# Products of the unit matrix in TensorE's queue, ahead of the first transposes and of those of ten early tiles

## The chip, the core and the metric

The kernel runs on one core of a Trainium2 chip. A core has five engines, each with its own queue of instructions that it takes in order: TensorE (PE in the profile; its weight loads are PEld) multiplies matrices, VectorE (DVE) and ScalarE (ACT) work element by element and can read the results of PE in PSUM, GpSimd (POOL) works element by element on SBUF, and SyncE (SP) issues the DMA transfers here. The metric is the time of one execution on the device, in microseconds, as the median of several runs.

## The reference

Attention with a threshold, followed by a two-layer network. The shapes are 8 batches, 8 heads, 576 rows and 64 columns per head; the network takes 4608 rows of 512, with a hidden width of 2048.

```python
scores = scale * np.matmul(q, k.transpose(0, 1, 3, 2))
thresh = np.max(scores, axis=-1, keepdims=True) - tau
scores = np.where(scores >= thresh, scores, -1000000000.0)
scores = scores - np.max(scores, axis=-1, keepdims=True)
attn = np.exp(scores)
attn = attn / (np.sum(attn, axis=-1, keepdims=True) + 1e-09)
x = np.matmul(attn, v)          # heads side by side: 4608 x 512
h = x @ w_in                    # 512 x 2048
g = np.maximum(h, 0.0) + np.log1p(np.exp(-np.abs(h)))
out = g @ w_out                 # 2048 x 512
```

## The kernel before

**Attention.** A unit is one batch and one pair of heads; there are 32 units of nine tiles of 128 query rows, so 288 tiles, numbered from 0. Each tile goes through the same steps. `scores` (line 425) multiplies on PE into one of two PSUM banks `s`; `row_max` (446) takes the largest score on DVE into `negm` and the threshold `thr`; `exps` (453) takes exponentials on ACT into `e_all`, which has room for two tiles; `mask` (457) drops what lies under the threshold on DVE and sums the row; `weights_T` (477) transposes the masked tile on PE against the unit matrix `ident`; `weights_hi` (512) copies the transposed tile out of PSUM on ACT into `gH`; `values` (561) multiplies by v on PE. For the first 36 tiles the transposes go into the pool of four PSUM banks with tag `g` (line 483), later into the tile's own bank of scores. Beside this the next unit's k and q are split into a rounded part and a rest on POOL (`hi_of`, `lo_of`, lines 124 to 133), transposed on PE (`qkT`, 370) and copied out by ACT; the halves of qT are swapped by DMA (lines 404 and 405).

**Weights.** w_in and w_out are 64-bit numbers in DRAM and arrive in pieces of 512 KB. `to_f32` (169) turns each piece into a pair of 32-bit words: DMA into `wc` (line 204), ACT takes the high word's size into `wa` (212), POOL clamps it (213), three DVE steps put the bits together (219 to 224), and POOL makes the rounded part and the rest (196 and 197). Pieces of w_in are then written back to DRAM as `wi_d` by DMA (line 253), and pieces of w_out stay in SBUF as `wo`. Each piece needs free buffers before its load can start.

**Network.** Nine chunks of 512 rows. `hidden` (651) makes the hidden layer in three products per block (lines 664, 666 and 668), ACT takes the softplus, and `project` (720) multiplies by w_out (line 732). The first chunk can start when the four units of batch 0, tiles 0 to 35, have stored their x.

**Order.** The loop at line 963 calls these steps tile by tile in the order of the letters of `PAT0` (tiles before 36) and `PAT` (after). That is the order in which the program is written down. Where each instruction then stands in its engine's queue is settled by the scheduler of the framework when the program is built: it places instructions by its own estimate of when each could run, within their dependencies and within the order that `behind` (143) adds as a dependency without a wait. So code that is added on one engine can move instructions on all of them.

Of the kernel before, what the change touches and what calls it, by code (L numbers as in the profile page):

```python
# [9 lines left out]
F32 = mybir.dt.float32  # L10
# [13 lines left out]
P = 128  # L24
# [9 lines left out]
PAT = "ThRlefmpfxSvwp"  # L34
PAT0 = "RMTeShlfpfxvwp"
WD = 4
ST = (1, 3, 4, 4, 5, 6, 6, 8)
VO = (1, 1, 1, 0)
RT = 1
# [21 lines left out]
def tile_kernel(ctx: ExitStack, tc: tile.TileContext, q, k, v, tau, w_in, w_out, out):  # L61
# [8 lines left out]
    nc = tc.nc  # L70
# [19 lines left out]
    ps_g = ctx.enter_context(tc.tile_pool(name="ps_g", bufs=GB, space=PSUM))  # L90
# [5 lines left out]
    identr = cpool.tile([P, P], F32R, name="identr")  # L96
# [41 lines left out]

    now = {"p": 0, "tile": 0}
    masked = []  # L140
    scored = []

    def behind(i, others):

        if others:
            tc.add_manual_dep(i.ins, others[-1].ins.name, mybir.DependencyInfo(
                mybir.DependencyClass.NoSync, mybir.DependencyReason.DATA), reason="order")
# [146 lines left out]
    for b in range(B):  # L294
        for kind in (("one", "two") if b < NSPLIT else ("all",)):
            for hp in range(NPAIR):
# [6 lines left out]
                for g, (j, members) in enumerate(groups):  # L303
                    c = 0
# [65 lines left out]
    def qkT(s, j, n):  # L370

        ps = ps_g.tile([P, 512], F32, tag="g", name=f"tr_{s.i}_{j}_{n}")
        pr = ps.bitcast(F32R)
        if n == 2:
            nc.tensor.transpose(pr[:, 0:P], s.k2[:, NC, :], identr)
            if j == 0 and s.kind != "one":
                nc.tensor.transpose(pr[:, P:2 * P], s.q2[0][:, NC, :], identr)
            defer(1, lambda: qkT_rest(s, j, ps))
            return
        cols = range(NC) if n == 0 else range(NC)[s.cols]  # L380
        for c in cols:
            src = s.k2[:, j * (NC + 1) + c, :] if n == 0 else s.q2[j][:, c, :]
            nc.tensor.transpose(pr[:, c * P:(c + 1) * P], src, identr)  # L383
        if n == 0:
            s.kT.append(apool.tile([P, S + SR], F32R, tag="kT", name=f"kT_{s.i}_{j}"))
            t = s.kT[j]
            defer(1, lambda: act.copy(t[:, SR:S], ps))
        else:
            t = [apool.tile([P, SM], F32R, tag=f"qT{i}", name=f"qT{i}_{s.i}_{j}") for i in range(2)]
            s.qT.append(t)  # L390
            w = slice(cols[0] * P, (cols[-1] + 1) * P)
            defer(1, lambda: queries(s, t[0][:, w], t[1][:, w], ps[:, w]))
# [32 lines left out]
    def scores(s, t):  # L425
        if t == s.tiles[0]:
            s.sums = apool.tile([P, 9], F32, tag="sums", name=f"sums_{s.i}")
            s.half, s.sp, s.m, s.grp = {}, {}, {}, {}
        sp = banks[nth[0] % SB]
        s.half[t] = half = nth[0] % 2  # L430
        nth[0] += 1
        s.sp[t] = sp
        if t == NC:
            parts = [(qm[:, n, j, :], j) for j in range(2) for n in range(2)]
        else:
            j = 0 if t < NC else 1
            c = t if t < NC else t - NC - 1
            parts = [(s.qT[j][n][:, c * P:(c + 1) * P], j) for n in range(2)]
        k0 = (1 - half) * SR
        for m, (lhs, j) in enumerate(parts):  # L440
            for hf in range(2):
                i = nc.tensor.matmul(sp[:, hf, 0:HS], lhs, s.kT[j][:, k0 + hf * HS:k0 + (hf + 1) * HS],  # L442
                                     start=(m == 0), stop=(m == len(parts) - 1))
        scored.append(i)

    def row_max(s, t):
        negm = apool.tile([P, 1], F32, tag="negm", bufs=3, name=f"negm_{s.i}_{t}")
# [22 lines left out]
    def mate(s, t):  # L470
# [3 lines left out]
        u = t if t < NC else t - 1  # L474
        return (t + 1, False) if u % 2 == 0 else (t - 1, True)

    def weights_T(s, t):
        half = s.half[t]
        e = e_all[:, half, :]
        other, second = mate(s, t)  # L480
        lone = other is None
        if 9 * NPAIR * s.b + 9 * s.hp + t < TG:
            main = ps_g.tile([P, NC, P], F32, tag="g", name=f"tm_{s.i}_{t}")
            rest = ps_g.tile([P, NC, P], F32, tag="g", name=f"tr_{s.i}_{t}")[:, 0, :] if lone or second else None
        else:
            sp = s.sp[t]
            main = sp[:, 0, :].rearrange("p (c n) -> p c n", n=P)
            rest = sp[:, 1, 0:P]
        if second:
            nc.tensor.transpose(rest, e_all.rearrange("p h n -> p (h n)")[:, SM:SM + P], ident)  # L490
        for c in range(NC):
            c0 = half * SR + c * P
            nc.tensor.matmul(main[:, c, :], e[:, c0:c0 + P], ident, is_transpose=True, start=True, stop=True)  # L493
        if lone:
            r0 = 0 if half else SM
            nc.tensor.transpose(rest[0:SR, :], e[:, r0:r0 + SR], ident)
        s.sp[t] = (main, rest)
# [53 lines left out]
    def slow_products():  # L551
        if not slow:
            return
        for f in slow[0][:3]:
            behind(f(), scored)
        del slow[0][:3]
        if not slow[0]:
            slow.pop(0)
            defer(1, ends.pop(0))
# [289 lines left out]
    chunks, first = [], []  # L849
# [26 lines left out]
    for kind, g in WL:  # L876
        for m in range(4):
            n = len(prep)
# [56 lines left out]


    u0 = units[0]
    for s in units:
        s.eng_lo = nc.gpsimd
    load(u0)  # L940
# [22 lines left out]
    for g, (cur, t) in enumerate(tiles):  # L963
# [6 lines left out]
        for step in PAT0 + ("m" if g == TG - 1 else "") if g < TG else PAT:  # L970
# [24 lines left out]
            elif step == "w":  # L995
                while prep and prep[0][0] <= g:
                    _, f, a = prep.pop(0)
# [42 lines left out]
```

## Time and profile before

| | |
|---|---|
| median of three runs | 1426.15 us (1426.09 to 1426.85) |
| profiled execution, its own time | 1425.26 us |
| its span, first to last instruction | 1423.5 us |
| PE busy | 1380.4 us, 97% of the span |
| DVE, ACT, POOL busy | 69%, 59%, 41% |
| granted TensorE clock, mean | 1.000 |

The page gives busy time per engine, the chain of work that ended last, and the costliest groups of instructions. The windows split the span into stretches, since a mean over the whole hides that the first 145 us, before the network starts, are a different stage from the rest. The timelines show single instructions with the idle time before them and what ended it. Names are those of the kernel's tiles without their numbers. Helpers record under one line: all DVE and ACT operations read as L156 and need their tile's name.

### The profile page before, as it was taken

Reading aid. Unit: us, or ns where it says so; the run is one execution under the profiler, and the core shown is the slowest. Engines: PE = TensorE matmul, PEld = TensorE weight load, DVE = VectorE, ACT = ScalarE, POOL = GpSimd, SP = SyncE. Lnnn points to the kernel's source line nnn. Section 1 sums busy time; section 2 is a strip of 40 time slices with the busy share of each in tenths; the row PEclk is TensorE's granted clock in tenths of the full one; section 3 lists DMA queues with packets and bytes.
Section 4 is the critical chain, followed back from the end, with each engine's and each line's share of the span. In section 5 each row is a group of like instructions: output and inputs, shape, how many; then the busy total and the mean of one; then the engine's idle time right before and its main releaser. Section 6 shows DMA issues by size and latency. Waiting matters only on the chain.

```text
span 1423.5 us, 23587 instructions
## 1 busy us (share of the span) xinstructions
PE 1380.4 (97%) x7860; PEld 1164.5 (82%) x7860; DVE 987.5 (69%) x2211; ACT 846.7 (59%) x1615; POOL 586.2 (41%) x619
## 2 busy tenths in 40 slices
PE   6987999999999999999999999999999999999998
PEld 5555688788888888888888888888888888788886
DVE  6988688787777777787778777877777777402111
ACT  5766767667666576667666666667666765221110
POOL 3666666543333433344334333344334431323221
PEclk9999999999999999999999999999999999999999
DMA  5766766435333534445443533453434532343421
GB/s 168 220 191 208 233 195 186 125 102 173 111 105 111 156 105 124 120 131 158 118 119 98 158 108 110 124 145 117 123 113 141 154 94 84 110 130 115 135 76 45
DMA packets 131209, 189.94 MB, mean 133 GB/s; under 512 B 35312, under 2 KB 86800, under 8 KB 131088
## 3 DMA queue, kind: packets, MB, share of 16 engines
q1 hardware_dynamic: 131088, 188.43, 45.4%
q8 instruction: 63, 1.03, 0.3%
q14 instruction: 58, 0.48, 0.1%
HBM read 140.51 MB, written 27.41 MB: 118 GB/s over the span
## 4 chain that ended last, share of the span: by engine, by line
PE 86%; DVE 4%; DMA 2%; issue 2%; POOL 2%; ACT 1%; SPq 1%; POOLq 0%; DVEq 0%; ACTq 0%
PE o L732 28%; PE s L442 11%; PE h L664 9%; PE h L666 9%; PE h L668 9%; PE s L493 7%; PE pv L574 4%; PE pv L575 4%; PE tr L383 2%; DVE e_all L156 1%; PE pv L576 1%; DVE negm L156 1%; PE s L490 1%; PE pv L568 1%; DMA wc_i<-in_moe_w_in_dram 1%
## 5 line engine op out<-in xcount | busy, mean ns | idle before, releaser
L732 PE MATMUL o<-wo_o,g 128*128 128x512 f32 x1728 | 446.4, 400 | 1.1 <-POOL g L133 1.1
L732 PEld LDWEIGHTS o<-wo_o,g 128*128 128x128 f32 x1728 | 313.7, 189 | 60.6 <-POOL g L133 2.1
L133 POOL TENSOR_TENSOR g<-st,g 128x512 fp32r<-128x512 f32 x144 | 189.8, 1338 | 240.4 <-DVE g L156 222.4
L156 DVE SCALAR_TENSOR_TENSOR e_all<-s,thr,e_all 128x576 f32<-128x576 f32 x288 | 235.2, 817 | 38.0 <-ACT e_all L156 33.4
L156 ACT CAST gH<-s 128x512 fp32r<-128x512 f32 (+2 forms) x432 | 179.5, 467 | 136.8 <-PE s L493 115.5
L156 ACT ACTIVATE e_all<-s,negm 128x576 f32<-128x576 f32 x288 | 215.8, 750 | 32.7 <-DVE negm L156 17.0
L664 PE MATMUL h<-xh,wi 128*128 128x512 f32 x576 | 232.6, 404 | 1.8 <-ACT xh L156 0.8
L156 DVE TENSOR_REDUCE negm<-s 128x1 f32<-128x576 f32 x288 | 215.2, 747 | 25.0 <-PE s L442 21.9
L666 PE MATMUL h<-xl,wi 128*128 128x512 f32 x576 | 231.6, 402 | 0.7 <-POOL xl L133 0.7
L668 PE MATMUL h<-xh,wi 128*128 128x512 f32 x576 | 229.2, 398 | 0.0
L156 DVE TENSOR_TENSOR gL<-s,gH 128x512 fp32r<-128x512 f32 (+1 forms) x270 | 169.0, 634 | 47.3 <-ACT gH L156 40.5
L442 PE MATMUL s<-kT,qT 128*128 128x288 f32 x1024 | 193.0, 311 | 8.1 <-ACT gH L156 4.1
L156 DVE CAST g<-st 128x512 fp32r<-128x512 f32 x128 | 58.8, 501 | 169.0 <-ACT st L156 169.0
L442 PEld LDWEIGHTS s<-kT,qT 128*128 128x128 f32 x1024 | 148.4, 191 | 24.6 <-ACT gH L156 5.3
L493 PE MATMUL s<-identr,e_all 128*128 128x128 f32 x1008 | 151.3, 273 | 0.2 <-DVE e_all L156 0.2
L156 ACT ACT_TABLE_LOAD x111 | 142.4, 1283 | 5.4 <-PE h L668 3.4
L156 ACT ACTIVATE st<-h 128x512 f32<-128x512 f32 x144 | 78.3, 595 | 112.5 <-PE h L668 111.8
L664 PEld LDWEIGHTS h<-xh,wi 128*128 128x128 f32 x576 | 108.5, 188 | 25.7 <-ACT xh L156 1.3
L493 PEld LDWEIGHTS s<-identr,e_all 128*128 128x128 f32 x1008 | 119.4, 140 | 10.9 <-DVE e_all L156 3.5
L666 PEld LDWEIGHTS h<-xl,wi 128*128 128x128 f32 x576 | 108.6, 188 | 22.2 <-POOL xl L133 1.5
L668 PEld LDWEIGHTS h<-xh,wi 128*128 128x128 f32 x576 | 108.5, 188 | 22.1
L574 PE MATMUL pv<-gH,vt 128*128 128x256 f32 (+1 forms) x432 | 118.3, 297 | 0.3 <-ACT gH L156 0.2
(94 smaller groups left out, 1830.0 us busy)
## 6 DMA issues: line engine op xcount, KB each, us to landing
wi<-wi_d SPq DMA_DIRECT2D x144, 512.0 KB
qT<-qT SPq DMA_DIRECT2D x124, 128.0 KB
R<-r_d SPq DMA_DIRECT2D x64, 144.0 KB
kn<-in_k_dram SPq DMA_DIRECT2D x32, 256.0 KB
qn<-in_q_dram SPq DMA_DIRECT2D x32, 256.0 KB
vn<-in_v_dram SPq DMA_DIRECT2D x32, 256.0 KB
wc_i<-in_moe_w_in_dram SPq DMA_DIRECT2D x16, 512.0 KB
wi_d<-wc_i SPq DMA_DIRECT2D x32, 256.0 KB
```

The lines of the kernel that those rows point to most:

```text
L133: eng.tensor_tensor(out=out_, in0=in_, in1=hi.bitcast(F32), op=ALU.subtract)
L156: i = getattr(self.eng, name)(*args, **kwargs)
L383: nc.tensor.transpose(pr[:, c * P:(c + 1) * P], src, identr)
L442: i = nc.tensor.matmul(sp[:, hf, 0:HS], lhs, s.kT[j][:, k0 + hf * HS:k0 + (hf + 1) * HS], start=(m == 0), stop=(m == len(parts) - 1))
L490: nc.tensor.transpose(rest, e_all.rearrange("p h n -> p (h n)")[:, SM:SM + P], ident)
L493: nc.tensor.matmul(main[:, c, :], e[:, c0:c0 + P], ident, is_transpose=True, start=True, stop=True)
L574: nc.tensor.matmul(o[:, 0:n], vt[:, c, :], h[:, c, 0:n], start=(c == 0), stop=False)
L575: nc.tensor.matmul(o[:, 0:n], vt[:, c, :], l[:, c, 0:n], start=False, stop=False)
L664: nc.tensor.matmul(h, wi[:, 0, cc, :], u.h[cc], start=(cc == 0), stop=False)
L666: nc.tensor.matmul(h, wi[:, 0, cc, :], u.l[cc], start=False, stop=False)
L668: nc.tensor.matmul(h, wi[:, 1, cc, :], u.h[cc], start=False, stop=(cc == NCC - 1))
L732: nc.tensor.matmul(o, u.g[fc][m // 2][:, sl], wo[fc][:, m % 2, :], start=(n == 0), stop=(n == 3 * QF - 1))
```

## The change

Two groups of new products and one rule of order are added. `in_use` multiplies the unit matrix by itself, four copies side by side (512 columns), and writes into a PSUM tile that is overwritten or never read. Eight such products stand ahead of the first transposes of k, with a PSUM tile of their own, `first`. For the ten tiles of the table `KEEP` a few stand ahead of the tile's transposes and write into the PSUM tile `main` that the transposes then fill: 8 for tile 0, 4 for tile 2, 3 for tile 5, then 2, 2, 4, 2, 4, 2 and 2 for tiles 14, 19, 23, 27, 30, 32 and 33. That makes 41 products. The list `at_PE` ties each product behind the scores, the transposes of k and q or the slow products that were written down before it.

```diff
+KEEP = {0: 8, 2: 4, 5: 3, 14: 2, 19: 2, 23: 4, 27: 2, 30: 4, 32: 2, 33: 2}
...
+    at_PE = []
...
-            nc.tensor.transpose(pr[:, c * P:(c + 1) * P], src, identr)
+            at_PE.append(nc.tensor.transpose(pr[:, c * P:(c + 1) * P], src, identr))
...
         scored.append(i)
+        at_PE.append(i)
...
+    def in_use(out_, n):
+
+        for _ in range(n):
+            i = nc.tensor.matmul(out_, identr, identr.unsqueeze(1).to_broadcast([P, 4, P]), start=True, stop=True)
+            behind(i, at_PE)
+            at_PE.append(i)
...
+        in_use(main.rearrange("p c n -> p (c n)"), KEEP.get(now["tile"], 0))
         if second:
...
         for f in slow[0][:3]:
-            behind(f(), scored)
+            i = f()
+            behind(i, scored)
+            at_PE.append(i)
...
     u0 = units[0]
+    in_use(ps_g.tile([P, 512], F32, tag="g", name="first"), 8)
```

The scheduler answers with other places on all five engines, from the start to about tile 42; behind that the queues read as before. Two places matter for the prediction.

**The start.** ACT's queue around the first exponentials, before. The names `e_all` are the exponentials of tiles 0 and 1, `qT0_0_1` is a copy of transposed q, and `wa_i0_0` is ACT's step on the first piece of w_in.

```order
L156 CAST kT_0_1_203<-tr_0_1_0_198 128x512
L156 CAST kT_0_1_203<-tr_0_1_2_205 128x2x64
L156 ACTIVATE qT0_0_1_213<-tr_0_1_1_208,qscale_88 128x512
L156 ACTIVATE e_all_141<-s_0_142,negm_0_0_223 128x576
L156 ACTIVATE e_all_141<-s_1_143,negm_0_1_236 128x576
L156 ACTIVATE wa_i0_0_254<-wc_i0_0_253 128x512
```

The same place after:

```order
L158 CAST kT_0_1_212<-tr_0_1_0_207 128x512
L158 CAST kT_0_1_212<-tr_0_1_2_214 128x2x64
L158 ACTIVATE wa_i0_0_271<-wc_i0_0_270 128x512
L158 ACTIVATE qT0_0_1_222<-tr_0_1_1_217,qscale_88 128x512
L158 ACTIVATE e_all_141<-s_0_142,negm_0_0_232 128x576
L158 ACTIVATE e_all_141<-s_1_143,negm_0_1_245 128x576
```

The step on the weight piece has moved from behind the first two exponentials to a place in front of them. SP's queue around the load of that piece, `wc_i0_0`, before:

```order
L325 DMA qn_1_188<-in_q_dram 64x64 x2
L328 DMA vn_1_232<-in_v_dram 128x2x256
L404 DMA qm_107<-qm_107 64x256
L405 DMA qm_107<-qm_107 64x256
L340 DMA vn_1_232<-in_v_dram 64x2x64 x2
L204 DMA wc_i0_0_253<-in_moe_w_in_dram 128x1024
```

The same place after:

```order
L327 DMA qn_1_197<-in_q_dram 64x64 x2
L330 DMA vn_1_241<-in_v_dram 128x2x256
L342 DMA vn_1_241<-in_v_dram 64x2x64 x2
L206 DMA wc_i0_0_270<-in_moe_w_in_dram 128x1024
L406 DMA qm_107<-qm_107 64x256
L407 DMA qm_107<-qm_107 64x256
L330 DMA vn_2_553<-in_v_dram 128x2x256
```

The load of the piece has passed the two swaps of `qm`, and the third unit's v stands behind it.

**Around tile 30.** POOL's queue, before. `wa_i2_1` and `wa_i2_2` are clamps of two pieces of w_in; `wc_i2_0` is the rounding of the piece ahead of them, `q2_4_0` and `k2_4` are splits of q and k of unit 4, and `wo_o3` is a piece of w_out.

```order
L126 TENSOR_SCALAR wo_o3_1064<-wa_o3_1063 128x512
L126 TENSOR_SCALAR q2_4_0_1339<-qn_4_1202 128x5x64
L133 TENSOR_TENSOR wo_o3_1064<-wa_o3_1063,wo_o3_1064 128x512
L133 TENSOR_TENSOR q2_4_0_1339<-qn_4_1202,q2_4_0_1339 128x5x64
L126 TENSOR_SCALAR wc_i2_0_1139<-wa_i2_0_1140 128x512
L133 TENSOR_TENSOR wc_i2_0_1139<-wa_i2_0_1140,wc_i2_0_1139 128x512
L534 MEMSET gH_3_1_1306 64x64
L213 TENSOR_SCALAR wa_i2_1_1216<-wa_i2_1_1216 128x512
L213 TENSOR_SCALAR wa_i2_2_1276<-wa_i2_2_1276 128x512
```

The same place after:

```order
L127 TENSOR_SCALAR wo_o3_1092<-wa_o3_1091 128x512
L134 TENSOR_TENSOR k2_4_1304<-kn_4_1233,k2_4_1304 128x9x64
L134 TENSOR_TENSOR wo_o3_1092<-wa_o3_1091,wo_o3_1092 128x512
L215 TENSOR_SCALAR wa_i2_1_1248<-wa_i2_1_1248 128x512
L127 TENSOR_SCALAR wc_i2_0_1171<-wa_i2_0_1172 128x512
L134 TENSOR_TENSOR wc_i2_0_1171<-wa_i2_0_1172,wc_i2_0_1171 128x512
L545 MEMSET gH_3_1_1340 64x64
```

The clamp of `wa_i2_1` now stands in front of the rounding of `wc_i2_0`, and the split of `q2_4_0` has gone further forward, out of these rows. SP's queue around the load of the next piece, `wc_i2_2`, before; `wi_d2` is the store of the piece `wc_i2_0`.

```order
L204 DMA wc_i2_1_1215<-in_moe_w_in_dram 128x1024
L328 DMA kn_5_1542<-in_k_dram 128x2x256
L325 DMA kn_5_1542<-in_k_dram 64x64 x2
L328 DMA qn_5_1543<-in_q_dram 128x2x256
L253 DMA wi_d2_92<-wc_i2_0_1139 128x4x128
L204 DMA wc_i2_2_1275<-in_moe_w_in_dram 128x1024
```

The same place after:

```order
L206 DMA wc_i2_1_1247<-in_moe_w_in_dram 128x1024
L330 DMA kn_5_1584<-in_k_dram 128x2x256
L327 DMA kn_5_1584<-in_k_dram 64x64 x2
L206 DMA wc_i2_2_1309<-in_moe_w_in_dram 128x1024
L255 DMA wi_d2_92<-wc_i2_0_1171 128x4x128 x2
L615 DMA r_d2_111<-rt_2_1314 9x128
```

The load `wc_i2_2` has passed a load of q and the store that waits for POOL's rounding of `wc_i2_0`.

## Rows read from the trace of the kernel before

**Rows 1.** The page: busy time of each engine, and the chain by engine.

```profile
PE 1380.4 (97%) x7860; PEld 1164.5 (82%) x7860; DVE 987.5 (69%) x2211; ACT 846.7 (59%) x1615; POOL 586.2 (41%) x619
...
PE 86%; DVE 4%; DMA 2%; issue 2%; POOL 2%; ACT 1%; SPq 1%; POOLq 0%; DVEq 0%; ACTq 0%
```

**Rows 2.** Windows: length; busy of PE, PEld, DVE, ACT, POOL; clock, DMA share, GB/s.

```profile
0.00:22.00 22.00, 9.79 (x46) 8.49 (x47) 11.78 (x30) 9.94 (x20) 5.36 (x13) 1.00 0.64 181
22.00:83.00 61.00, 55.00 (x330) 38.04 (x329) 55.17 (x114) 44.99 (x103) 38.02 (x46) 1.00 0.73 211
83.00:120.00 37.00, 28.91 (x174) 19.82 (x173) 29.49 (x63) 25.05 (x62) 25.62 (x30) 1.00 0.59 166
120.00:145.00 25.00, 19.83 (x106) 12.42 (x107) 19.72 (x40) 18.04 (x41) 18.88 (x22) 1.00 0.73 223
145.00:185.00 40.00, 37.87 (x197) 27.10 (x195) 26.80 (x50) 27.12 (x49) 25.11 (x27) 1.00 0.80 245
185.00:1395.00 1210.00, 1205.16 (x6916) 1039.52 (x6915) 838.27 (x1906) 720.49 (x1343) 470.16 (x481) 1.00 0.43 124
```

**Rows 3.** Timeline of PE: start, length, line, operation, idle before and its releaser.

```profile
16.23 1.11 PE L493 MATMUL tm<-identr,e_all 128*128 128x128 f32 x4 [3.62 <-DVE e_all L156]
17.00 1.31 PE L442 MATMUL s<-kT,qT 128*128 128x288 f32 x4
...
108.36 0.33 PE L490 MATMUL tr<-identr,e_all 128*128 128x128 f32 x1 [1.83 <-DVE e_all L156]
108.52 0.60 PE L493 MATMUL tm<-identr,e_all 128*128 128x128 f32 x4
108.88 0.78 PE L442 MATMUL s<-kT,qT 128*128 128x288 f32 x4
```

**Rows 4.** Timeline of PE, the run of equal products at the end.

```profile
1399.80 19.00 PE L732 MATMUL o<-wo_o,g 128*128 128x512 f32 x82
```

**Rows 5.** Timeline of ACT, the first exponentials and weight pieces.

```profile
12.28 0.69 ACT L156 ACTIVATE qT<-tr,qscale 128x512 fp32r<-128x512 f32 x1 [2.24 <-PE tr L383]
12.87 1.36 ACT L156 ACTIVATE e_all<-s,negm 128x576 f32<-128x576 f32 x2
17.96 0.67 ACT L156 ACTIVATE wa_i<-wc_i 128x512 f32<-128x512 f32 x1 [3.73 <-DMA wc_i<-in_moe_w_in_dram]
...
22.28 0.66 ACT L156 ACTIVATE wa_i<-wc_i 128x512 f32<-128x512 f32 x1 [1.53 <-DMA wc_i<-in_moe_w_in_dram]
```

**Rows 6.** Timeline of SP's queue: start and length of each issue.

```profile
10.95 0.50 SPq L404 DMA_DIRECT2D qm<-qm  x1
11.49 0.59 SPq L405 DMA_DIRECT2D qm<-qm  x1
...
13.50 0.59 SPq L204 DMA_DIRECT2D wc_i<-in_moe_w_in_dram  x1
```

**Rows 7.** Timeline of DVE, the first mask.

```profile
15.35 0.82 DVE L156 SCALAR_TENSOR_TENSOR e_all<-s,thr,e_all 128x576 f32<-128x576 f32 x1
```

**Rows 8.** Waits of DVE from 83 to 120: total us, times, longest.

```profile
DVE wa_i L156 <- POOL wa_i L213: 5.8, 4, 1.8
DVE wa_o L156 <- POOL wa_o L213: 1.6, 2, 1.2
```

**Rows 9.** Timeline of DVE, three of those waits.

```profile
105.75 0.43 DVE L156 TENSOR_SCALAR wa_i<-wa_i 128x512 uint32<-128x512 uint32 x1 [1.83 <-POOL wa_i L213]
...
110.22 0.43 DVE L156 TENSOR_SCALAR wa_i<-wa_i 128x512 uint32<-128x512 uint32 x1 [1.20 <-POOL wa_i L213]
...
119.36 0.43 DVE L156 TENSOR_SCALAR wa_i<-wa_i 128x512 uint32<-128x512 uint32 x1 [1.14 <-POOL wa_i L213]
```

**Rows 10.** Timeline of ACT, a piece that is waited for.

```profile
108.82 0.67 ACT L156 ACTIVATE wa_i<-wc_i 128x512 f32<-128x512 f32 x1 [3.38 <-DMA wc_i<-in_moe_w_in_dram]
```

**Rows 11.** Timeline of SP's queue, the issue of that piece.

```profile
103.90 0.50 SPq L204 DMA_DIRECT2D wc_i<-in_moe_w_in_dram  x1
```

**Rows 12.** Timeline of POOL, the clamp before it.

```profile
105.10 0.61 POOL L213 TENSOR_SCALAR wa_i<-wa_i 128x512 f32<-128x512 f32 x1
```

## The prediction, made before the changed kernel ran

> **What bounds the kernel now.** I read the page first. PE is busy for 1380.4 of 1423.5 us and holds 86% of the chain [rows 1], so the kernel as a whole waits for PE. The next view has to say where the other 43 us lie, since products that fill idle time can only matter there. The windows answer: PE is idle for 12.2 us of the first 22, for 6.0 from 22 to 83, 8.1 from 83 to 120, 5.2 from 120 to 145, 2.1 from 145 to 185, and for only 4.8 in the 1210 us after that [rows 2]. From 185 on PE is never short of work, so whatever comes before it reaches the end as a shift: a microsecond won or lost in the first 145 us is one at the end.
>
> In that early stage PE follows DVE. DVE is busy for 55.17 of 61 us and then for 29.49 of 37 [rows 2]. Of its 7.5 idle us from 83 to 120, 7.4 are waits for POOL's clamp of a weight piece [rows 8]. So three things count: how soon the first tiles start, how fast PE goes in them, and how much DVE waits for weight pieces.
>
> **PE's rate at the start.** Four transposes take 1.11 us at 16.23 and four score products 1.31 us at 17.00; the same groups take 0.60 and 0.78 us at 108.52 and 108.88 [rows 3]. So PE runs at about half its rate in the first tiles. The granted clock reads 1.00 (the 2.4 GHz level) in the first window too [rows 2], but durations decide, and these are what the 1.2 GHz level would give.
>
> **The products themselves.** There are 41: 8 at the front and 33 from the table. At PE's full rate one of 512 columns takes 19.00 / 82 = 0.232 us [rows 4], at half rate twice that, 0.46. The first 8 need 1.9 to 3.7 us. They need only the unit matrix, while the transposes behind them wait for k to be loaded and split, and PE's first 22 us hold 12.2 idle ones [rows 2]. The next 8 lie in the wait of 3.62 us ahead of tile 0's transposes [rows 3]. The 21 for tiles 5 to 33 come to 21 x 0.232 = 4.9 us, against 14.1 us of PE idle from 22 to 120 [rows 2]. They need the same PSUM tile as the transposes behind them, and where the wait ended with DVE's mask the tile was free before; tile 30, with four products (0.93 us), had 1.83 us of idle in front [rows 3]. So I cost all 41 at nothing; with all cover gone in the late tiles the price is 4.9.
>
> **What they bring.** If the front products have PE at full rate by tile 0, the transposes and scores of two tiles shorten: 2 x (0.51 + 0.53) = 2.1 us on the way from mask to mask.
>
> **The start: ACT now waits for the first weight piece before the first exponentials.** This is a cost, and the diff does not show it. Before, ACT copied the second half of q at 12.28, took both exponentials from 12.87, and only then waited for the weight piece, which it had at 17.96; the first mask began at 15.35 [rows 5, 7]. In the new order the step on the piece stands ahead of all three. Its load was issued at 13.50 and landed 17.96 - 13.50 = 4.46 us later [rows 5, 6]. It now passes the two swaps of `qm` (10.95 to 12.08, 1.1 us [rows 6]), so it starts at 12.4 and lands at 16.8. ACT's step takes 0.67, the copy of q 0.59 (12.28 to 12.87), and an exponential 1.36 / 2 = 0.68 [rows 5]: the first is done at 18.7. The first mask starts 3.4 us later than at 15.35 [rows 7]. Bounds: if the load lands before ACT wants it, nothing is lost; if it takes 2 us longer, 5.4. I take 3.4, as the row is of the same load on the same queue.
>
> Of these 3.4 us PE's full rate gives back 2.1. The next piece is asked for about a microsecond sooner too, and ACT waited 1.53 us for that one [rows 5], but it now has another piece to wait for behind it, so I count only 0.3. What is left at tile 4 is +1.0, between -2 (no wait for the piece) and +3.4 (no faster PE).
>
> **Tiles 20 to 35: weight pieces a place further ahead.** DVE waited 1.83, 1.20 and 1.14 us for clamps at 105.75, 110.22 and 119.36 [rows 9], together 4.2. Each has a cause that the new order takes away. At 105.10 the clamp ran on POOL behind the rounding of the piece before it [rows 12]; now it stands in front of that, about 2 us sooner. The piece for 110.22 was issued at 103.90, behind a store that waits for POOL, and ACT stood 3.38 us for it until 108.82 [rows 10, 11]; now its load is in front of that store and of a load of q. The third clamp stood behind the scaling of x and a split, and ACT's step for it now comes a tile earlier. The two waits for pieces of w_out, 1.6 together [rows 8], lose a part, since their clamps no longer stand behind a small fill that waits for PE. The remaining wait (5.8 - 4.2 = 1.6) stays: its load keeps its place behind the copies of q.
>
> With all five gone the gain would be 4.2 + 0.9 = 5.1. But DVE then meets the next thing that is late, the exponentials, which wait for the transposes of the tile before. How much that is can be read where no clamp was late: from 22 to 83 DVE was idle for 5.83 of 61 us, 9.6% [rows 2]. At that share the 37 us would hold 3.5 instead of 7.5, a gain of 4.0. I take 4.6, between the two; the ends are 0 and 7.4.
>
> **Tiles 36 to 42.** Here four products of the hidden layer move in front of a tile's scores, and one transpose of a tile in front of the next tile's scores. PE is idle for 5.2 us from 120 to 145 [rows 2], so both can fill a hole or hold up the scores behind them. I take 0, and +-2 for the range.
>
> **Sum.** +1.0 - 4.6 + 0 = -3.6 us. The profiled execution took 1425.26 us, so 1421.7; the median of the runs stands 0.9 above that execution, which makes 1422.5.
>
> **A rule that would give another result.** The trace shows full durations for the transposes at 108.52, right after an idle 1.83 us [rows 3], and the granted clock reads 1.00 in all windows [rows 2]; so at the later tiles there is no slow rate to lift, and their 21 products bring nothing. The Trainium skill, "TensorE: Matmul & The Clock Gate", section on HAM oscillation, says that waits between bursts of matmuls can put the engine back to half rate again and again, and that keeping it busy avoids this. By that rule the products at tiles 14 to 33 would be the point of the change. Were it so in executions without the profiler, each of these eight tiles would win what the first two do, 1.04 us: 8.3 us, a time of 1414.2. The rows contradict it, so it has a small chance.
>
> **Rivals.**
> 1. *The lead of the weight pieces brings nothing, and the kernel is as before.* For it: ACT waits for exponentials and loads all through this stage, so a clamp that is early may only show that the exponentials are late. Then 1426.15 + 1.0 - 1.0 for a part of the waits: 1426.
> 2. *Slower, by the wait on ACT.* The mechanism is the load of the first piece, and behind it each next piece that ACT meets before the exponentials of tiles 3 and 4. If these loads land later than I reckon, since they share the DMA engines with v and k of the third unit, tile 4 is late by 3.4 and the lead of the pieces is eaten up as well: 1426.15 + 3.4 = 1429.6. It decides from a landing of the first piece after about 18 us. Against it: the bytes in front of each piece hardly change.
> 3. *The front gain survives.* The first piece lands before ACT wants it, or PE's rate helps more tiles: -2 at tile 4, then -4.6: 1419.5. Against it: the load takes 4.46 us in the trace.
>
> **How the numbers follow.** Forecast 0.50, rival 1 0.20, rival 2 0.17, rival 3 0.10, the rule 0.03. 0.2% of 1426 is 2.85 us, about what can be told from no change. The forecast's own range is 1419 to 1426, with some two thirds of it under 1423.3; that with rival 3 and the rule gives 0.46 for faster. The rest of the forecast and rival 1 give 0.37 for the same, rival 2 gives 0.17 for slower. The range, 1417 to 1429, takes in rivals 1 and 3 and nearly reaches rival 2.
>
> **What would show it.** Right: transposes of tile 0 at about 0.6 us for four; ACT idle until about 16.8 for the first weight piece, with the first mask near 18.7; no waits of DVE for POOL near 105, 110 and 119; PE's first product of the hidden layer 2 to 4 us sooner than before. Wrong: a first mask before 16 or after 20; DVE as idle from 83 to 120 as before; or slow transposes behind the idle times of the later tiles in a trace in which the products are left out.

## The result and the profile after

The changed kernel is slower. Ratios in this part are time over the time of the kernel before, in runs on the same chip, with a 95% interval.

| | before | after |
|---|---|---|
| median of 6 runs, us | 1427.03 (1426.09 to 1430.54) | 1434.22 (1431.82 to 1436.60) |
| ratio | | 1.0048 (1.0033 to 1.0064) |
| profiled execution, us | 1425.26 | 1434.96 |
| its span, us | 1423.5 | 1433.2 |
| mean granted clock of that execution | 1.000 | 0.993 |

The prediction was 1422.5 with a range of 1417 to 1429. The kernel went the other way, and its time lies outside that range.

The windows of after have the columns of [rows 2]. From 185 on PE is nearly as full as before (2.1 us less busy, which the part on the end takes up), so most of the loss lies in front of it. From 22 to 120 PE is busy for 6.4 us more than before, by the added products and by work at half rate, while DVE is busy for 83.4 us against 84.7. The clock column, 1.00 throughout before, is below 1.00 in three windows.

```profile
0.00:22.00 22.00, 12.99 (x48) 9.86 (x49) 9.09 (x23) 8.38 (x16) 5.04 (x12) 0.78 0.66 192
22.00:83.00 61.00, 57.33 (x327) 40.16 (x327) 53.24 (x114) 43.99 (x100) 37.39 (x46) 0.97 0.70 194
83.00:120.00 37.00, 33.00 (x194) 23.04 (x193) 30.12 (x65) 26.06 (x64) 24.61 (x29) 1.00 0.61 182
120.00:145.00 25.00, 19.85 (x106) 12.51 (x105) 19.19 (x39) 15.17 (x34) 18.23 (x22) 1.00 0.82 234
145.00:185.00 40.00, 36.77 (x180) 25.61 (x179) 22.95 (x48) 28.49 (x55) 24.68 (x27) 0.96 0.69 204
185.00:1395.00 1210.00, 1203.05 (x6911) 1037.61 (x6910) 839.75 (x1911) 721.98 (x1345) 470.96 (x483) 1.00 0.43 125
```

To find where the time goes I set the start of each tile's mask on DVE, read from the timeline, against the same mask before. The columns of the runs belong to the experiments below; each is from one profiled execution. How far two executions of one kernel differ shows a second profile of the kernel before (e11): by this measure it lies within 0.5 us of the first up to tile 8, but 1.63 us behind it at tile 26 and 1.38 at tile 88. So differences of up to 1.6 us behind the first tiles cannot be told from a second execution, and what a kernel costs is read from the medians.

| tile | before, us | after | front only (e2) | order alone (e5) | tiles only (e1) | order kept (e6) | piece sooner (e9) | late piece (e13) | both pieces (e14) |
|---|---|---|---|---|---|---|---|---|---|
| 0 | 15.35 | +4.77 | +4.85 | -0.67 | +0.07 | +0.18 | +0.04 | +4.77 | -0.13 |
| 4 | 26.57 | +4.35 | +5.75 | +6.96 | +0.88 | +0.66 | +2.09 | +4.27 | +3.89 |
| 26 | 92.40 | +3.45 | +5.18 | +4.26 | -0.01 | +0.02 | +0.27 | +3.39 | +3.20 |
| 35 | 122.75 | +3.07 | +6.32 | +5.00 | +0.85 | -0.02 | -0.59 | +3.98 | +3.01 |
| 36 | 126.33 | +4.59 | +6.53 | +5.19 | +0.18 | +0.42 | +2.17 | +3.96 | +3.00 |
| 37 | 130.09 | +3.19 | +5.22 | +3.91 | -0.34 | +0.78 | +0.78 | +2.88 | +1.92 |
| 43 | 153.92 | +4.11 | +9.54 | +7.51 | -0.03 | +1.08 | +5.07 | +3.78 | +4.98 |
| 44 | 160.24 | +5.94 | +9.93 | +7.44 | -0.12 | +0.77 | +6.89 | +4.05 | +6.37 |
| 50 | 192.75 | +6.55 | +10.17 | +7.67 | +0.30 | +1.14 | +7.12 | +4.28 | +6.62 |
| 88 | 359.11 | +6.56 | +10.03 | +6.54 | +1.14 | +0.99 | +5.96 | +3.92 | +6.46 |

In after, 4.4 us are lost by tile 4 and some 1.3 come back by tile 35. At tile 36 the mask is 1.5 us later again, of which 1.4 are made up at tile 37; by tile 43 the lag is 4.1, and 1.8 go between tiles 43 and 44. From tile 50 to the last tile the lag stays within 6.4 to 7.2 us, close to the 7.2 between the medians.

**The start.** ACT's timeline of after, to be read against [rows 5]: the piece lands at 16.94, as forecast, but it stands in front of the second copy of q too, and so does DVE's half of that copy, which stands in front of the first mask (DVE, second fence, against [rows 7]). That step of 1.51 us is not in the forecast.

```profile
16.94 0.66 ACT L158 ACTIVATE wa_i<-wc_i 128x512 f32<-128x512 f32 x1 [6.84 <-DMA wc_i<-in_moe_w_in_dram]
17.50 0.68 ACT L158 ACTIVATE qT<-tr,qscale 128x512 fp32r<-128x512 f32 x1
18.07 1.37 ACT L158 ACTIVATE e_all<-s,negm 128x576 f32<-128x576 f32 x2
21.27 0.67 ACT L158 ACTIVATE wa_i<-wc_i 128x512 f32<-128x512 f32 x1 [1.83 <-DMA wc_i<-in_moe_w_in_dram]
```

```profile
18.21 1.51 DVE L158 TENSOR_SCALAR qT<-tr,qscale 64x512 fp32r<-64x512 f32 x2 [4.74 <-ACT qT L158]
20.12 0.82 DVE L158 SCALAR_TENSOR_TENSOR e_all<-s,thr,e_all 128x576 f32<-128x576 f32 x1
```

PE's timeline of after, against [rows 3]. The products at the start do bring the full rate: four transposes take 0.53 us at 6.62. By 9.21 four score products take 1.33 again, the half rate. The eight products of tile 0 end at 15.98 (12.48 + 3.50); then PE stands for 5.02 us, and tile 0's transposes take 1.11 us, just as before. In e4, one of the experiments, PE waits only 0.33 us behind the same eight products, and the transposes take 0.66 us (second fence). So in after the effect of these eight was spent on the wait.

```profile
1.71 3.78 PE L483 MATMUL first<-identr 128*128 128x512 f32 x8 [1.71 <-POOL identr L98]
6.62 0.53 PE L385 MATMUL tr<-identr,k 128*128 128x128 f32 x4 [1.13 <-DVE k L158]
9.21 1.33 PE L444 MATMUL s<-kT,qT 128*128 128x288 f32 x4 [0.58 <-ACT qT L158]
12.48 3.50 PE L483 MATMUL tm<-identr 128*128 128x512 f32 x8
21.00 1.11 PE L504 MATMUL tm<-identr,e_all 128*128 128x128 f32 x4 [5.02 <-DVE e_all L158]
```

```profile
16.34 0.66 PE L507 MATMUL tm<-identr,e_all 128*128 128x128 f32 x4 [0.33 <-DVE e_all L159]
```

**Tiles 20 to 35.** DVE's waits from 83 to 120 in after, against [rows 8]. The three at 105.75, 110.22 and 119.36 [rows 9] are gone, as forecast, and the waits for POOL fell from 7.4 to 3.8. But waits for ACT's exponentials came, and one for a clamp grew to 2.6.

```profile
DVE wa_i L158 <- POOL wa_i L215: 2.6, 1, 2.6
DVE e_all L158 <- ACT e_all L158: 1.8, 3, 0.9
DVE wa_o L158 <- POOL wa_o L215: 1.2, 1, 1.2
DVE negm L158 <- PE s L444: 0.7, 2, 0.5
```

**Tile 36.** The same lead sends a piece of w_out on ACT in front of the exponentials of tile 36, where its load has not landed (ACT, then DVE, in after). Before, that piece stood behind the exponentials of tile 37. The mask of tile 37 looks as if the wait were made up, but the work that leads to x has kept it, as the next part shows.

```profile
129.59 0.67 ACT L158 ACTIVATE wa_o<-wc_o 128x512 f32<-128x512 f32 x1 [2.87 <-DMA wc_o<-in_moe_w_out_dram]
130.16 0.72 ACT L158 ACTIVATE e_all<-s,negm 128x576 f32<-128x576 f32 x1
```

```profile
130.92 0.82 DVE L158 SCALAR_TENSOR_TENSOR e_all<-s,thr,e_all 128x576 f32<-128x576 f32 x1 [2.50 <-ACT e_all L158]
```

**Tiles 43 to 44.** PE's product of the hidden layer waits for ACT's copy of x, which waits for its load: 1.58 us at 157.40 in after (first fence), 0.77 at 151.84 before (second). Behind it stands a stretch at a lower granted clock. The windows (third fence: busy, clock, DMA share, GB/s) give 1.96 x 0.12 + 4.00 x 0.31 = 1.5 us of PE's work lost; before shows 1.00 in all of it (in 144 to 172 us).

```profile
157.40 0.50 PE L677 MATMUL h<-xh,wi 128*128 128x512 f32 x1 [1.58 <-ACT xh L158]
```

```profile
151.84 0.50 PE L664 MATMUL h<-xh,wi 128*128 128x512 f32 x1 [0.77 <-ACT xh L156]
```

```profile
156.00:160.00 4.00, 1.96 (x7) 0.88 0.60 206
160.00:164.00 4.00, 4.00 (x17) 0.69 0.83 254
```

Why the load of x is late can be followed back. The last x of the first chunk needs the row sums of the fourth unit (tiles 27 to 35). PE transposes them (`rT`), ACT copies them out, they go through DRAM, POOL multiplies by them, and only then is x stored (`x_d`) and loaded again. The two fences show `rT` on PE and the issue of the store on SP, before and then after: 4.97 and 4.63 us later, while the mask of tile 35 is only 3.07 later. In every trace but that of e4 the product that needs x starts 20.2 to 23.0 us behind `rT`.

```profile
131.57 0.27 PE L595 MATMUL rT<-identr,rs 128*9 128x128 f32 x1
...
144.75 1.77 SPq L616 DMA_DIRECT2D x_d<-xp  x3
```

```profile
136.54 0.27 PE L608 MATMUL rT<-identr,rs 128*9 128x128 f32 x1
...
149.38 1.76 SPq L629 DMA_DIRECT2D x_d<-xp  x3
```

**The end.** The span is 9.7 us longer, the lag of the tiles 6.5. The other 3.2 come after 1230: PE waits 2.12 us at 1239.05 for POOL, and the next 4 us run at a mean clock of 0.64.

```profile
1239.05 0.50 PE L745 MATMUL o<-wo_o,g 128*128 128x512 f32 x1 [2.12 <-POOL g L134]
```

```profile
1240.00:1244.00 4.00, 3.72 (x10) 0.64 0.36 86
```

### The profile page after: what moved, and what is told of

It reads as the page before. It is cut to its first block, busy times and chain, and to the rows that moved or that the text cites. A ratio compares the mean times of both kernels' runs of the same rounds, so it can differ in the third digit from the quotient of the medians.

```text
span 1433.2 us, 23674 instructions
## 1 busy us (share of the span) xinstructions
PE 1396.5 (97%) x7901; PEld 1175.7 (82%) x7901; DVE 982.1 (69%) x2211; ACT 846.2 (59%) x1615; POOL 586.1 (41%) x619
## 4 chain that ended last, share of the span: by engine, by line
PE 84%; DVE 3%; ACT 2%; DMA 2%; issue 2%; POOL 1%; SPq 0%; DVEq 0%; ACTq 0%; POOLq 0%
PE o L745 26%; PE s L444 11%; PE h L677 9%; PE h L679 9%; PE h L681 9%; PE s L504 7%; PE pv L587 4%; PE pv L588 4%; PE tr L385 2%; DMA wc_o<-in_moe_w_out_dram 1%; PE pv L589 1%; PE s L501 1%; DVE e_all L158 1%; DVE negm L158 1%; PE pv L581 1%
```

## The experiments

**Products or order?** Theory A: the loss comes from the new order of the queues, which the eight products at the start bring about. Theory B: it comes from the products. Four products at the start leave ACT's and POOL's order as it was, five give that of the changed kernel (no run has five), so the two can be separated.

The products of the tiles without those at the start:

```diff
-    in_use(ps_g.tile([P, 512], F32, tag="g", name="first"), 8)
```

> All 33 products in front of the tiles' transposes, but not the eight at the start; the queues of ACT, POOL and SP then stand as before, and DVE's differ in two places of neighbouring instructions. Theory A (the loss of 7 us comes from the new order of the queues, which the eight products at the start bring about): 1423 to 1428 us, at most 2 us from before. Theory B (the loss comes from the products themselves, which take PE time and hold PSUM tiles in front of the transposes): 1431 us or more, and masks of tiles 0 to 4 that start 2 us or more later than before.

Measured: 1428.74 us (12 runs), 1.0009 (1.0000 to 1.0018). The time is 0.7 us above A's range and 1.4 above before's median on that chip; the mask of tile 4 is 0.88 late, not over 2. For A.

The products at the start alone:

```diff
-KEEP = {0: 8, 2: 4, 5: 3, 14: 2, 19: 2, 23: 4, 27: 2, 30: 4, 32: 2, 33: 2}
+KEEP = {}
```

> The eight products at the start alone, none at the tiles; the queues of ACT, POOL and SP stand nearly as in the changed kernel, with the first weight piece in front of the second qT and the exponentials on ACT. Theory A: 1431 to 1437 us, with the mask of tile 0 some 4.8 us later than before, as in the changed kernel. Theory B: 1425 to 1429 us, since 33 of the 41 products are gone.

Measured: 1436.50 us (6 runs), 1.0059 (1.0045 to 1.0073), mask of tile 0 at 20.20. The whole loss is there with 33 of 41 products gone. For A.

The order with no product at all, in the kernel before:

```diff
+            if name == "i0_0":
+                behind(second_qT[1], [i])          # i: ACT's step on the first piece
...
+        if s.i == 0 and t == s.tiles[0]:
+            behind(i, second_qT[:2])               # i: the exponentials
```

> No product at all; ties in the program's order put ACT's work on the first weight piece and the second qT in front of the first exponential, as they stand in the changed kernel, and the later order of the queues follows close to that of the run with the eight products at the start alone. Theory A (the order makes the loss): 1432 to 1438 us, mask of tile 0 at 19.5 to 20.5 us, and 6 us or more behind before by tile 50. Theory B (the products make it): 1425 to 1429 us.

Measured: 1433.74 us (6 runs), 1.0056 (1.0039 to 1.0073). Tile 0's exponentials stayed in front of the piece, so its mask is at 14.68 and that expectation missed; tile 1's are behind it, with the mask at 20.91. From tile 66 to 88 the lag is 6.5 us, as in the changed kernel, without one product; at tile 4 it is 6.96 against 4.35, so the two orders are alike and not the same. Theory A holds: an order of this kind costs the time without any product. ACT's rows and PE's product of the hidden layer repeat what after shows:

```profile
18.09 0.66 ACT L159 ACTIVATE wa_i<-wc_i 128x512 f32<-128x512 f32 x1 [3.45 <-DMA wc_i<-in_moe_w_in_dram]
```

```profile
158.32 0.50 PE L682 MATMUL h<-xh,wi 128*128 128x512 f32 x1 [3.39 <-ACT xh L159]
```

**The products with the order put back.** Four at the start in place of eight, the rest as changed:

```diff
-    in_use(ps_g.tile([P, 512], F32, tag="g", name="first"), 8)
+    in_use(ps_g.tile([P, 512], F32, tag="g", name="first"), 4)
```

> As the changed kernel, but four products at the start in place of eight; ACT, POOL then have the order of before, and SP but for some neighbouring loads of the first 25 us. Theory A: 1422 to 1428 us, with the mask of tile 0 within 1 us of 15.35. Theory B: 1431 to 1436 us, since 37 of the 41 products stay.

Measured: 1425.26 us (11 runs), 0.9993 (0.9977 to 1.0008): no difference that can be measured. Tile 0's mask is at 15.57. The mask of tile 2 is 1.26 us earlier than before, that of tile 4 0.16 later; in between ACT waits for the next two pieces:

```profile
21.59 0.67 ACT L158 ACTIVATE wa_i<-wc_i 128x512 f32<-128x512 f32 x1 [1.94 <-DMA wc_i<-in_moe_w_in_dram]
...
25.41 0.66 ACT L158 ACTIVATE wa_i<-wc_i 128x512 f32<-128x512 f32 x1 [2.03 <-DMA wc_i<-in_moe_w_in_dram]
```

All 41 products, with ACT's step on the first piece tied behind an exponential, in two places (the newest one at that point, then tile 1's):

```diff
+            if name == "i0_0":
+                behind(i, weighed)        # weighed: the exponentials so far; the next run: weighed[:2]
```

> As the changed kernel with all 41 products, but ACT's work on the first weight piece is tied behind an exponential, so that it no longer stands in front of the second qT; the later order of the queues is then a third one, neither that of before nor that of the changed kernel. Theory A with the piece as its cause at the start: the mask of tile 0 at 14.5 to 16.5 us in place of 20.1, 4 us of the loss gone, 1428 to 1432 us. Theory B: the mask of tile 0 stays over 18.5 us and the time at 1432 to 1437 us.

> All 41 products; ACT's work on the first weight piece is tied behind the exponentials of tile 1, after which the queues of ACT and POOL stand as before, those of DVE and SP nearly. Theory A: 1422 to 1427 us; masks of tiles 2 and 3 some 1.3 us earlier than before, since the products of tile 0 bring PE to its full rate, and that gain gone again by tile 4, where ACT waits for the next weight pieces. Theory B: 1431 to 1436 us.

Measured: 1428.23 us (12 runs), 1.0007 (0.9998 to 1.0017), mask of tile 0 at 15.46; and 1430.42 us (11 runs), 1.0026 (1.0018 to 1.0035). The first is for A, and as its order is a third one, it also shows that not every new order is a loss. The second misses A's range by 3.4 us, though its profiled execution (1427.95, the lowest of its eleven) lags by only 1.0 at tile 88: with the order kept the products are no gain. Why this version is 0.26% slower no trace here shows.

With the second and third piece behind the exponentials of tiles 3 and 4 as well, then the same with 16 of the products:

```diff
+            behind(i, weighed[:{'i0_0': 2, 'i0_1': 4, 'i0_2': 5}.get(name, 0)])
-KEEP = {0: 8, 2: 4, 5: 3, ...                  (second of the two)
+KEEP = {0: 8}
```

> As the run before it (41 products, first piece behind tile 1's exponential), with ACT's work on the second and the third weight piece tied behind the exponentials of tiles 3 and 4. If the landing of the pieces is what takes the gain of the start back: tile 4's mask 1 to 2.2 us earlier than before, kept to tile 26, and the time 1 to 2 us under the run before it (1421 to 1425 us). If the pieces' later steps on DVE and POOL set the pace anyway: the gain is gone by tile 36 and the time within 1 us of that run.

> As the run before it, with the products at the start and in front of tile 0's transposes alone (16 of 41). If the products of the later tiles cost nothing and gain nothing: within 0.1% of that run. If those of tiles 23 to 33 help PE at tiles 27 to 40, as the shift of -0.6 to -1.7 us there in the run with four products at the start may say: 1 to 2 us slower than that run. If they hold PE up: as much faster.

Measured: 1427.13 us (11 runs), 1.0006 (0.9993 to 1.0019), and 1427.37 us (12 runs), 1.0005 (0.9992 to 1.0018). The time of the first is 3.3 us under the run before it, more than expected, yet above the expected 1421 to 1425. The pieces did cap the gain: tile 4 is 1.63 us earlier in the first run, tile 35 still 1.54. But it does not reach the end. PE's first product behind the load of x starts at nearly the same time as before (151.59 against 151.84), with the gain turned into a wait:

```profile
151.59 0.50 PE L679 MATMUL h<-xh,wi 128*128 128x512 f32 x1 [1.81 <-ACT xh L159]
```

Behind it PE's rate falls (mean clock 0.70 from 152 to 156, 0.87 to 160), and by tile 44 the kernel is 0.62 late, which is within what two executions of before differ by. The 25 other products change nothing that can be measured.

**What in the order costs the time?** The changed kernel with one row of SP moved, so that the first piece lands some 5.7 us sooner; all other engines keep its order:

```diff
+        if name == "i0_0":
+            for x in unit_1:               # the loads of the second unit
+                behind(x, [i])             # i: the transfer of the first piece
...
+            if name == "i0_0":
+                behind(i, kT_copies[:2])   # i: ACT's step; its place stays
```

> The changed kernel with one row moved: the transfer of the first weight piece is issued six rows earlier on SP, at about 6.7 us in place of 12.2, in front of the second unit's loads; PE, DVE, ACT and POOL keep the changed kernel's order. If ACT's wait for that piece makes the loss at the start: mask of tile 0 at 15 to 17 us in place of 20.1, and with it 3 to 4.5 us less in all, 1429 to 1431 us; what is left over before is then the later order's. If the order costs by something else than this wait: the mask of tile 0 stays over 18.5 us and the time at 1432 to 1437 us.

Measured: 1433.57 us (10 runs), 1.0044 (1.0028 to 1.0059). Tile 0's mask is back at 15.39 and tile 35 is 0.59 us ahead of before, yet the time does not move: my expectation of 3 us less failed. The next rows on ACT say why. The second piece, now waited for 4.90 us, and the piece of w_out, 4.12, are met earlier and still land late. The first of these waits shows at tile 4 (+2.09) and is made up by tile 35; the second is not:

```profile
11.28 0.68 ACT L160 ACTIVATE wa_i<-wc_i 128x512 f32<-128x512 f32 x1 [1.21 <-DMA wc_i<-in_moe_w_in_dram]
19.17 0.66 ACT L160 ACTIVATE wa_i<-wc_i 128x512 f32<-128x512 f32 x1 [4.90 <-DMA wc_i<-in_moe_w_in_dram]
...
127.17 0.66 ACT L160 ACTIVATE wa_o<-wc_o 128x512 f32<-128x512 f32 x1 [4.12 <-DMA wc_o<-in_moe_w_out_dram]
```

PE, idle behind that wait, then runs at half rate, and again at 160 (windows: busy, clock, DMA share, GB/s):

```profile
128.00:132.00 4.00, 1.75 (x6) 0.66 0.75 190
132.00:136.00 4.00, 4.00 (x12) 0.50 0.82 277
...
160.00:164.00 4.00, 4.00 (x12) 0.57 0.57 158
```

So two more runs, with that piece of w_out put back behind the exponentials of tile 37: in the changed kernel, and together with the sooner transfer.

```diff
+            behind(i, weighed[:{'o5': 38}.get(name, 0)])
```

> The changed kernel with one of its later moves undone: ACT's work on one w_out piece, which stands in front of the exponentials of tile 36 and waited 2.87 us for its transfer, is tied behind those of tile 37, where the kernel before has it. PE's order stays the changed kernel's, two rows each move on DVE, ACT and POOL. The wait at the start (mask of tile 0 at 20.1 us) stays. Theory C (the waits of ACT for this piece and for the first one make the loss, each by itself): the mask of tile 36 comes 1.5 to 2.5 us earlier against tile 35's than in the changed kernel, and the time 1431 to 1433 us. Theory D (the later order as a whole makes it): 1433 to 1436 us.

> The run with the first piece's transfer issued sooner, and with the w_out piece tied behind tile 37's exponentials as well: all 41 products and the changed kernel's order, without either of the two waits. Theory C: masks of tiles 36 to 39 within 1 us of before's, no stretch at half the granted clock at 128 to 136 us, and 1425 to 1429 us. Theory D: 1431 us or more, with tiles 36 to 44 losing 4 us or more again.

Measured: 1432.13 us (12 runs), 1.0030 (1.0015 to 1.0045), and 1430.57 us (12 runs), 1.0020 (1.0004 to 1.0036). In the first the mask of tile 36 follows that of tile 35 without the 1.5 us that after loses there (+3.98, +3.96), and the lag at the end of the stage falls from 6.55 to 4.28. The time lies in C's range. The second is in neither range: it is the fastest with this order, but not as fast as before. Its stretch at half clock at 128 to 136 is gone, but the masks of tiles 36 to 39 are 1.9 to 3.5 us behind before's, where C had them within 1. The second piece still costs it 5.75 us of ACT's time at the start, and the load of x 2.78 at 158.28:

```profile
20.14 0.66 ACT L161 ACTIVATE wa_i<-wc_i 128x512 f32<-128x512 f32 x1 [5.75 <-DMA wc_i<-in_moe_w_in_dram]
```

```profile
158.28 0.50 PE L693 MATMUL h<-xh,wi 128*128 128x512 f32 x1 [2.78 <-ACT xh L161]
```

What the w_out piece's wait costs is best read at `rT`, on the way to x. There, against tile 35's lag, after loses another 1.90 us and e9 5.33, but e13, e14, e2 and e5, where ACT does not wait at that piece (0.32 us in e5), lose only 0.68 or 0.69 each. So the wait, with the slower PE behind it, is worth 1.2 us in after and 4.6 in e9, and it falls on x. The fall of the lag at the end from 6.55 to 4.28 is more than that: 1.6 us of it come between tiles 43 and 44, where the granted clock falls in after (0.88, 0.69) and stays at 1.00 in e13's one trace, an execution 2.9 us faster than its median.

Theory C is right in that these waits cost, and too narrow: each wait taken away shows the next one of its kind. The medians bear out less than the traces: e13's interval overlaps widely with after's (1.0033 to 1.0064) and e14's by a little, so what each wait by itself is worth in time is not shown.

**Versions that might win, and the kernel before once more.** Four products and the first piece's transfer issued early; the early transfer without products; and four products at the start and tile 0's eight, with every other row of PE, DVE, ACT and POOL as before:

```diff
+            for x in unit_1:
+                behind(x, [i])
...
-KEEP = {0: 8, 2: 4, 5: 3, ...                  (third of the three, with 4 at the start)
+KEEP = {0: 8}
```

> Four products at the start and the 33 at the tiles, the first piece's transfer issued early and its work on ACT tied behind tile 1's exponential, so that ACT and POOL have the order of before. With the piece early, ACT's waits for the second and third piece stay. Gains at the start are then 0.5 to 2 us at tile 4; if the load of x for the feed-forward stage, which PE waits for at 151 to 152 us, caps every gain: 1424 to 1428 us, no better than the run with four products alone.

> No product; the kernel before with only the first piece's transfer issued early on SP. If the products gain something beside the early transfer, this is slower than the run with four products and the early transfer by 0.5 to 2 us; if not, the same within 0.1%. Against before: 1425 to 1428 us.

> Twelve products: four at the start, eight in front of tile 0's transposes; PE, DVE, ACT and POOL have the order of before word for word otherwise, SP but for neighbouring loads of the first 25 us. If what the products do for PE's rate is worth something in the end: masks of tiles 2 and 3 some 0.7 to 1.3 us earlier and 1424 to 1426 us. If the gain of the start is taken back by the next weight pieces and the load of x, as in the runs with the order kept: masks within 0.5 us of before from tile 4 on, and 1426 to 1428 us.

Measured: 1429.98 us (12 runs), 1.0006 (0.9995 to 1.0018); 1427.12 us (11 runs), 0.9993 (0.9984 to 1.0002); 1429.80 us (12 runs), 1.0021 (1.0011 to 1.0030). None beats the kernel before. The first misses its range by 2 us. The second, without products, was expected 0.5 to 2 us slower than the first if the products gain something, and within 0.1% if not; it is 2.9 us (0.2%) faster, which is neither, and no gain of the products. The third was expected at 1428 or less and is slower by 0.2%, though its profiled execution (1427.29, the lowest of its twelve) leads by 0.8 us at tile 88. What its other executions lose is not in that trace.

> The kernel before itself, profiled once more. If the 3.2 us that the changed kernel's profile loses after 1230 us belong to an execution and not to a kernel, this profile shows a wait over 0.5 us or a granted clock under 1.00 in the last 250 us, which the first profile of before does not.

Measured: 1427.58 us. PE waits 0.71 us near 1232 there (0.41 in the first profile), with no fall of the clock: its end is 0.9 us longer than the first profile's, not 3.2. In the other runs the end adds 0.3 (e8) to 4.3 us (e1, whose order is nearly that of before). So those 3.2 us depend on the execution at least in part; how much is the kernel's stays open.

## Why the prediction was wrong

The forecast had tile 50 at -3.6 us; it is at +6.55. The 10.15 us between them divide into 3.35 by tile 4 (steps 2 and 3: +1.0 forecast, +4.35 measured), 3.32 from tile 4 to 35 (step 4: -4.6 and -1.28), 0.88 from tile 35 to 42 (step 5: 0 and +0.88), and 2.60 behind tile 42, for which the forecast had no term.

**(1) The products cost nothing.** Nearly. The cover was worked out for 37 of the 41; the four of tile 2 were left out. With the order kept, versions with 12 to 41 products come out between 0.9993 and 1.0026, two of seven clearly above 1 (e6 and e15). The 4.9 us named as the price without cover bounds it; what sets it within that range is open.

**(2) PE's rate helps the first two tiles, -2.1.** The mechanism was right and its cover was not. With ACT free of the wait, tile 2 is 1.1 to 1.3 us earlier (e3, e6, e7, e8), about half of the 2.1. In the changed kernel the wait of step 3 left PE idle for 5.02 us between the products and tile 0, and the rate was gone. This is the first step that failed: I added a gain and a loss that exclude each other.

**(3) The start, +3.4, of which +1.0 stays at tile 4.** The landing was right (16.8 against 16.94). The size was off: the mask of tile 0 came 4.77 us later, since DVE's 1.51 us on q stand in front of it, and of this only 0.4 was given back: +4.35 at tile 4. A first mask after 20 us was the prediction's own sign for this.

**(4) Weight pieces a place further ahead, -4.6.** This is the largest term of the sum, and the second step that failed. The three waits are gone as forecast, but tiles 27 to 34 gained 2.0 us (lag 4.74 to 2.74), not 4.6, and the clamp wait that grew to 2.6 had cost 1.3 at tile 27 (3.45 to 4.74). What DVE met next were exponentials (1.8 us of waits) and scores (0.7). And a piece that goes further ahead on DVE and POOL goes further ahead on ACT too, while its transfer does not land sooner: ACT's wait of 2.87 us for the piece of w_out costs 1.2 us at `rT`. I priced the wait removed and not the load that is late next.

**(5) Tiles 36 to 42, 0 within 2.** By tile 42 the lag has grown by 0.9 us, so the term holds as far as it goes. What it does not hold is the way to x: `rT` is 4.97 us late, and PE's product of the hidden layer, which I had 2 to 4 us sooner, came 5.6 later (151.84 to 157.40). The wait in front of it and the fall of the clock behind it make 1.8 us between tiles 43 and 44.

**The rivals.** Rival 2 named the right engine, the right queue and the right kind of wait; at 1429.6 its price was half of what it is. Its reason (loads that land later) is not what happened: the first load landed on time, and ACT met the later ones too early. Rival 1's view, that early clamps may only show that something else is late, is in part what after shows: the waits for clamps fell by 3.6 us, and waits for exponentials and scores, 2.5, took their place.

The rule on TensorE's rate had a chance of 0.03. The traces do show PE at the lower of its two levels behind idle stretches (granted clock 0.50 from 20 to 24 us in after and e13, from 132 to 136 in e9, from 160 to 164 in e2), so it was wrong to rule this out by the 1.00 column of one trace. The Trainium skill, "TensorE: Matmul & The Clock Gate", section on HAM oscillation, describes this; the runs agree that it happens, and show that here products in front of later tiles do not turn it into a gain (e7 against e8: 1.0006 and 1.0005). The sum under that rule counted eight tiles from 14 to 33; there are seven, and eight only with tile 5.

What stays open: the last 0.2% of e14, why e6 and e15 cost 0.2% while e3, e7 and e8 do not, and how the 7.2 us between the medians divide among the waits.

## What to carry to other kernels

- Where a scheduler sets the order, a cheap addition on an engine with idle time can still cost: compare the order of every queue, and for each step that moves ahead ask when its transfer lands, on each engine that touches it.
- Test such a change as two: the added work with the old order, and the new order without the work. Here that took three runs (1.0009, 1.0059, 1.0056) and was decisive.
- A gain in an early stage is worth what the next transfer lets through: 1.5 us at tile 35 became a wait for x at 151.6.

## What the runs showed of the hardware

- The lower clock is more than a matter of the start. Behind idle stretches of 1.6 to 3.4 us in front of the product at 157 to 158 us (1.58 in after, 3.39 in e5, 2.78 in e14), the granted clock from 160 to 164 us fell to between 0.60 and 0.73, at 1.3 to 1.7 us of PE's work a time; behind the 0.77 at 151.84 before it stayed 1.00, and so it did behind 2.28 us at 151.63 in e3 and 2.39 at 154.80 in e10: the idle stretch alone does not tell.
- In the first 20 us of the kernel before, the clock column reads 1.00 while durations are 1.7 to 1.9 times those at 108 us (1.31 against 0.78 us, 1.11 against 0.60 [rows 2, 3]); after, with products from 1.71, the same column shows 0.78. Durations are the safer witness there.
